# Three passes over 96 MLP units as two full matmuls and one quarter matmul in its own row group, and the last bias added by accumulating transfers

## The chip, the cores and the metric

One core of a Trainium2 chip runs the whole kernel. The metric is the time of one execution on the device in microseconds (us), as the median of several runs. The engines are named as in the profile: PE is the matrix engine (TensorE), PEld its weight loads, DVE the vector engine, ACT the scalar engine, POOL GpSimd, and SP the engine whose queue issues every transfer of the kernel before.

## The reference

`x` is 2048 tokens by 512. The block adds three things: `x`, a linear attention over the normalised `x` with 32 heads, and an MLP over the plain `x` with 1376 hidden units and a squared ReLU.

```
def _A_ref(x, wqkv, wo):
    qkv = ...(x @ wqkv)...
    q, k, v = qkv[0], qkv[1], qkv[2]
    phi = lambda t: jnp.where(t > 0, t + 1, jnp.exp(t)) + 1e-6
    pq, pk = phi(q), phi(k)
    kv = jnp.einsum("bhsd,bhse->bhde", pk, v)
    z = jnp.einsum("bhsd->bhd", pk)
    num = jnp.einsum("bhqd,bhde->bhqe", pq, kv)
    den = jnp.einsum("bhqd,bhd->bhq", pq, z)[..., None] + 1e-6
    o = num / den
    return ... o.reshape(B, S, D) @ wo

def _B_ref(x, w1, b1, w2, b2):
    h = jnp.einsum("bsd,df->bsf", x, w1) + b1
    zero = jnp.zeros_like(h)
    r = jnp.where(h > zero, h, zero)
    h = r * r
    out = jnp.einsum("bsf,fd->bsd", h, w2) + b2
    return out

x = A_x
xn = _layernorm(x, axis=-1)
return x + _A_ref(xn, A_wqkv, A_wo) + _B_ref(xn, B_w1, B_b1, B_w2, B_b2)
```

The last line gives the MLP the normalised `x` as well. The change touches only the second product of the MLP, `h @ w2 + b2`, and there only the last 96 of the 1376 units.

## The kernel before

**Split numbers.** Each 32-bit operand of a large product is held as two fp32r tiles, a high part (the rounded number) and a low part (what rounding left). A product is three matmuls, or passes, into the same PSUM bank: high by high, high by low, low by high (`PASSES`, `three`, lines 122 to 128). The high part is copied by ACT, the low part is a subtraction on DVE (`split`, `rest_of`).

**Tiling.** The 2048 tokens are 16 tiles of 128, in four blocks of four (`TB`). The 1376 units are 11 chunks of 128 (`NF`); chunk 10 has only 96 units (`FL`). In the kernel before, row 96 of chunk 10 carries `b2`: its weight in `w2` is `b2` and its hidden value is 1, because its bias in `b1s` is 1 and its column of `w1` is zero. Rows 97 to 127 are zero. So chunk 10 costs as much as a full chunk.

**Stages.** First the keys and values of all 16 tiles. Then two rounds of a loop over `n`, each for two blocks, `t1` and `t2`. A round computes the hidden units of both blocks at once by a seven-product scheme over pairs of chunks (the loop over `p`, lines 909 to 992). Inside that loop the second MLP product of block `t1` runs too, chunk by chunk, into four PSUM banks `acc`, one for each tile (`mlp_2`): chunk 10 opens the banks at `p == 0`. The hidden units of `t2` wait in `r2`. Then block `t1` gets its attention product (`add_attention`, 12 matmuls a tile), the sum with the residual on DVE (`add`) and its store. After it a loop over `e` (lines 1036 to 1064) takes nine waiting chunks of `t2`, four `add_attention` follow, and the two last chunks, `last_two` (0 and 10), close the banks. In the very last tile of the program the last two chunks go into two separate half banks (`end`, 256 columns each), so that half of the tile can leave while the other half is computed.

**Weights.** `w1` and `w2` are loaded piece by piece into six `raw` buffers. `piece_2` loads 128 rows of `w2`, and returns the two operations that make its high and low part (ACT, then DVE). The list `w2next` holds them, and `next_2`, `high_2` and the loop over `e` run them at fixed places. Chunk 10 of `w2` is loaded and split three times in the program, chunk 10 of `w1` (`raw_1`) twice.

**Order.** The program's text is the order of each engine's queue (`manual_schedule`): an instruction waits in its queue until its inputs are there and its output place is free, and everything behind it on that engine waits too. `hidden_2` squares the hidden units and splits them (ACT, ACT, DVE). `wait_for` does that for a chunk of `r2`. `load_res` loads `x` of a block as the residual, two tiles for each transfer, into `res`.

Of the kernel before, what the change touches and what calls it, by code (L numbers as in the profile page):

```python
# [7 lines left out]
F32 = mybir.dt.float32  # L8
F32R = mybir.dt.float32r
AF = mybir.ActivationFunctionType  # L10
# [8 lines left out]
def kernel(  # L19
# [43 lines left out]
    NP = NF // 2  # L63
    FP = NF * P
    FL = F - (NF - 1) * P
    assert D == 512 and S % BT == 0 and FL % 32 == 0 and FL < P

    nc.scalar.preload_act_table_set("natural_log_exp_and_others")

# [9 lines left out]
    def w512(name, tag, bufs):  # L79
        return work.tile([P, 512], F32, name=name, tag=tag, bufs=bufs)  # L80
# [65 lines left out]
    ident = keep.tile([P, P], F32, name="ident")  # L146
# [23 lines left out]
    def piece_q(j, eh, el):  # L170
        t = raw(f"rq{j}", chunk(wqkv, j, 0, D))
        g4 = lambda ap: ap.rearrange("p (g j c) -> p g j c", g=NJ, j=NJ)
        return lambda: split(g4(wq[0][:, j, :]), g4(wq[1][:, j, :]), gjc(t), eh, el)

    def raw_1(f):
        n = min(P, F - f * P)
        t = w512(f"r1_{f}", "raw", 6)
        tj = t.rearrange("p (j n) -> p j n", j=NJ)
        if n < P:
            nc.gpsimd.memset(tj[:, :, n:], 0.0)  # L180
        nc.sync.dma_start(tj[:, :, :n], w1[:, f * P:f * P + n].rearrange("(j p) n -> p j n", j=NJ))
        return t

    w2r = []
# [7 lines left out]

    def piece_2(f, at):

        if f < NF - 1:
            t = raw(f"r2_{f}", w2[f * P:(f + 1) * P, :])
        else:
            t = w512(f"r2_{f}", "raw", 6)
            nc.gpsimd.memset(t[FL:, :], 0.0)  # L199
            nc.sync.dma_start(t[:FL, :], w2[f * P:, :])  # L200
            nc.sync.dma_start(t[FL:FL + 1, :], b2[None, :])
        w2s[f] = [w2r[at // 2][:, at % 2 * 2 + u] for u in range(2)]
        h, l = w2s[f]
        return [lambda: copy("act", h, t), lambda: rest_of(l, t, h)]


    def group(*tiles):
# [225 lines left out]
    def hidden_2(name, r):  # L433
# [3 lines left out]
        split(s[:, 0], s[:, 1], r, "act", "dve")  # L437
        return s

    def relu(o, i, f):  # L440
        nc.scalar.activation(o, i, AF.Relu, bias=b1s[:, f:f + 1])  # L441

# [14 lines left out]
    def mlp_2(acc, f, s, first=False):  # L457
        for k in range(TB):
            three(acc[k], [s[:, u, k * P:(k + 1) * P] for u in range(2)], w2s[f], first, False)

    def add_attention(acc, i, last=False):
        t = aT.pop(i)
# [29 lines left out]
    nc.gpsimd.memset(b1s[:, NF - 1:], 0.0)  # L492
    nc.gpsimd.memset(b1s[FL:FL + 1, NF - 1:], 1.0)
    groups = {}
    x4, x8 = four("x4", "r1"), four("x8", "r2")
    for i0 in range(0, NT, TB):
# [150 lines left out]
    for i in range(2, NT):  # L647
        if i == NPE:
            wq = both("wq", ("B0", "B1"))
        if i == 3:  # L650
            nc.sync.dma_start(b1s[:, :NF - 1], b1[:(NF - 1) * P].rearrange("(f p) -> p f", p=P))
            nc.sync.dma_start(b1s[:FL, NF - 1:], b1[(NF - 1) * P:, None])
        move()
        fetch()
        ps = pks[i] if i < 3 else bank(f"pk{i}")
        if i > 2:
            project(i, ps, wk, HL)
        high = low = keep_t = lambda: None
        if i + 1 < NDVE:
            high, low, keep_t = transposed(i + 1)  # L660

        soon_turned = transposed(i + 2) if 11 <= i and i + 2 < NT else ()

        def late():
            if soon:
                roots(*soon)
            low()

        phi_k(i, ps, high, late)
        run(*soon_turned)  # L670
        later = normalise(*soon) if soon else []
        parts(i)
        keep_t()
        if i == 2:
            tokens(2)
        if i + 1 < NT:
# [12 lines left out]
        kx(i - 1)  # L689
# [100 lines left out]
    for n in range(2):  # L790
# [100 lines left out]
        t5, res = None, {}  # L891

        def load_res(t):
            for k in range(2):
                r = two(f"res{t}_{k}")
                i = t * TB + 2 * k
                nc.sync.dma_start(r, xf[i * P:(i + 2) * P, :].rearrange("(i p) d -> p i d", i=2))
                for i in range(2):
                    res[t, 2 * k + i] = r[:, i, :]

        def add(ps, t, k, a=0, z=D):
            r = res[t, k]
# [6 lines left out]
        for p in range(NP + 1):  # L909
# [5 lines left out]
                product(A, A11, [x[:, :2] for x in x1], True)  # L915
            if p:
                nc.vector.tensor_tensor(out=t5, in0=before, in1=t5, op=OP.add)
            if 0 < p < NP:
                chunk_split(1, 0, s34)
            if p:  # L920
                relu(r2[fb - 2], t5, fb - 2)
            if p < NP:
                c11 = w512(f"c11_{n}_{p}", "p", 6)
                copy("act", c11, A)
                product(B, A12, [x[:, 2:] for x in x1], True, True)
                high_2()
                nc.vector.tensor_tensor(out=c11, in0=B, in1=c11, op=OP.add)
                relu(c11, c11, fa)
# [15 lines left out]
            t5 = t5_  # L944
            if p == 0:
                T.update({k: tokens_sum(k, f"B{k - 3}") for k in (3, 4)})
                def last_sums(k):
                    for f in (difference_high, difference_low):
                        for j in range(2):
                            f(k, j, o34[k - 3][:, j])  # L950

                last_sums(3)
# [24 lines left out]
            nc.vector.tensor_tensor(out=c12, in0=C, in1=c12, op=OP.add)  # L977
            high_2()
            if p == 0:
                last_sums(4)  # L980
            relu(r2[fa], c12, fa)
            next_2(2 * p + 2)
            if p:
                mlp_2(acc, fb - 2, s.pop(fb - 2))
            else:
                mlp_2(acc, NF - 1, s.pop(NF - 1), True)
            if p == TB - 1:
                do(at1)
                move(16)
            product(A, S3, [T[3][:, u] for u in range(2)])  # L990
            if p == 2:
                load_res(t1)

        def wait_for(f):
            s[f] = hidden_2(f"s{n}_{t2}_{f}", r2[f])

        def sum_2(acc, k, f, first, stop, a=0, z=D):
            three(acc, [s[f][:, u, k * P:(k + 1) * P] for u in range(2)],
                  [w2s[f][u][:, a:z] for u in range(2)], first, stop)

# [35 lines left out]
        for e, f in enumerate(waiting[:-2]):  # L1036
            mlp_2(acc, f, s.pop(f), e == 0)
            if e + 3 < NF - 2:
                wait_for(waiting[e + 3])
            move(4)  # L1040
            if n == 0 and e == 3:
                f2 = xT[t2 - 2] = four(f"xt{t2 - 2}", "r3")
                nc.sync.dma_start(f2, xTd[t2 - 2])
            if e:
                do(w2next, 2)
                if e + 8 < NF:
                    g = waiting[e + 8]
                    w2next.extend(piece_2(g, place(g)))
            if e == 2:
                load_res(t2)  # L1050
            if 0 < e < 5:
                do(columns_todo)
            if e == NF - 6 and n == 0:
                wq = both("wr", ("B0", "B1"))
            if e == NF - 5:
                attention_places("ra", "r1")
                attentions_T(t2 * TB, t2 * TB + 1)
                fetch()
            if e == NF - 4:
                turned = attention_T(t2 * TB + 2)  # L1060
                pieces(1)
            if e == NF - 3:
                run(turned, attention_T(t2 * TB + 3))
                pieces(1)
        for k in range(TB):
            add_attention(acc, t2 * TB + k, n == 1 and k == last)
            if k < 2:
                wait_for(last_two[k])
                pieces(1)
            do(columns_todo)  # L1070
        if n == 1:
            add(acc[last], t2, last)
        for k in range(TB):
            if n == 1 and k == last:
                for a in (0, D // 2):
# [38 lines left out]
```

## Time and profile before

| what | value |
|---|---|
| median of 3 runs | 422.67 us (422.57 to 422.84) |
| the profiled execution, its own time | 422.49 us |
| its span, first to last instruction | 420.8 us |
| granted TensorE clock | 1.000 |
| PE busy | 99% of the span, 1860 matmuls |
| PEld busy | 82% |
| DVE busy | 70% |
| ACT busy | 60% |
| POOL busy | 7% |
| moved by transfers | 46.16 MB, mean 110 GB/s |

How to read it: a busy time of PE overlaps itself, since one matmul begins before the one ahead has drained. The distance from one matmul to the next is therefore read from the chain of waits, where a stretch of matmuls that follow each other is one line: start, length, engine, tile, line and count. Lines of the timeline show start, length, engine, line, operation, output and inputs, count, and in brackets how long the engine was idle before and what ended that. Groups of instructions end with busy us, mean ns of one, and idle time before. An issue of a transfer is shown with its kilobytes and the median time from issue to landing.

### The profile page before, as it was taken

The page shows a single profiled execution, that of the slowest core. Times are in us where ns is not written, and L with a number is a line of the kernel's source. Part 1 is how long each engine was busy: PE and PEld are TensorE (multiplying, and loading weights), DVE is VectorE, ACT ScalarE, POOL GpSimd, SP SyncE. Part 2 cuts the span into 40 slices and gives each one's busy share as a digit, 9 for nine tenths or more (in the row PEclk, how much of TensorE's full clock was granted, in tenths as well). Part 3 has the DMA queues.
Part 4 walks back from the last instruction along what each step waited for, and adds up shares of the span by engine and source line. Part 5 has one row for each costly group of instructions (what it writes and reads, how often), then busy time and mean ns, then how long its engine had stood idle before and what let it go on. Part 6 is the DMA issues. An engine that isn't in the chain of part 4 may idle for free.

```text
span 420.8 us, 5373 instructions
## 1 busy us (share of the span) xinstructions
PE 415.2 (99%) x1860; PEld 343.6 (82%) x1860; DVE 294.2 (70%) x536; ACT 254.0 (60%) x451; POOL 27.6 (7%) x50
## 2 busy tenths in 40 slices
PE   7999999999999999999999999999999999999996
PEld 7788888888887888888888888888888888888885
DVE  6886767777578877677579475586967667577343
ACT  5867777675467767665457362676667665546230
POOL 3242222220000000000000000000000000000000
PEclk9999999999999999999999999999999999999999
DMA  7885422800412231645026652401120654024502
GB/s 240 286 243 157 130 89 92 278 15 3 112 50 77 75 100 26 199 82 169 0 85 191 173 196 97 124 0 50 51 75 25 202 101 149 2 95 97 152 0 100
DMA packets 44818, 46.16 MB, mean 110 GB/s; under 512 B 5716, under 2 KB 31060, under 8 KB 44536
## 3 DMA queue, kind: packets, MB, share of 16 engines
q1 hardware_dynamic: 44792, 45.84, 36.5%
q8 instruction: 14, 0.23, 0.2%
q14 instruction: 12, 0.10, 0.1%
HBM read 32.71 MB, written 8.91 MB: 99 GB/s over the span
## 4 chain that ended last, share of the span: by engine, by line
PE 98%; DVE 1%; DMA 1%; ACT 0%; issue 0%
PE acc L128 39%; PE b L453 23%; PE kx L380 10%; PE pk L361 10%; PE pq L361 10%; PE pz L128 1%; PE b L128 1%; PE pkv L773 1%; PE pm L128 1%; DMA x<-in_A_x_dram 1%; PE pt L300 1%; PE end L128 0%; DVE st L214 0%; DVE xp L253 0%; DVE res L903 0%; ACT xs1h L316 0%
## 5 line engine op out<-in xcount | busy, mean ns | idle before, releaser
L128 PE MATMUL acc<-w2r,s 128*128 128x512 f32 x498 | 116.6, 389 | 0.0
L128 PEld LDWEIGHTS acc<-w2r,s 128*128 128x128 f32 x498 | 93.5, 188 | 19.6
L453 PE MATMUL b<-T,aop 128*128 128x512 f32 x240 | 59.6, 389 | 0.0
L453 PEld LDWEIGHTS b<-T,aop 128*128 128x128 f32 x240 | 45.0, 188 | 9.4
L380 PE MATMUL kx<-pk,tok 128*128 128x512 f32 x192 | 46.8, 392 | 0.0
L380 PEld LDWEIGHTS kx<-pk,tok 128*128 128x128 f32 x192 | 35.6, 188 | 7.9 <-DVE pk L369 0.6
L128 PE MATMUL acc<-mh,aTsr 128*128 128x512 f32 x96 | 30.3, 390 | 0.0
L109 ACT ACTIVATE w2r<-r 128x512 fp32r<-128x512 f32 x32 | 20.0, 625 | 13.8 <-PE acc L128 11.3
L120 DVE TENSOR_TENSOR w2r<-r,w2r 128x512 fp32r<-128x512 f32 x32 | 21.9, 685 | 7.3 <-ACT w2r L109 7.2
L453 PE MATMUL b<-xs0h,aop 128*128 128x512 f32 x80 | 26.4, 391 | 0.0
L117 POOL TENSOR_TENSOR tok<-xp,tok 128x512 fp32r<-128x512 f32 x16 | 21.7, 1362 | 54.9 <-ACT tok L109 54.9
L117 DVE TENSOR_TENSOR s<-c,s 128x512 fp32r<-128x512 f32 x20 | 13.8, 692 | 16.3 <-ACT s L109 16.3
L356 DVE SCALAR_TENSOR_TENSOR q<-pq,q 128x512 f32<-128x512 f32 x16 | 11.0, 689 | 14.9 <-ACT q L354 14.9
L109 ACT ACTIVATE aop<-S 128x512 fp32r<-128x512 f32 x20 | 12.6, 629 | 14.6 <-DVE S L702 9.4
L128 PEld LDWEIGHTS acc<-mh,aTsr 128*128 128x128 f32 x96 | 18.0, 188 | 3.8
L903 DVE TENSOR_TENSOR res<-acc,res 128x512 f32<-128x512 f32 x16 | 11.0, 692 | 14.2 <-PE acc L128 14.2
L352 ACT ACTIVATE q<-pq 128x512 f32<-128x512 f32 x16 | 9.4, 591 | 18.5 <-PE pq L361 18.5
L199 POOL MEMSET r<- 32x512 f32 x3 | 1.6, 522 | 278.2 <-DVE w2r L120 272.3
L128 PE MATMUL acc<-ml,aTsr 128*128 128x512 f32 x48 | 18.7, 390 | 0.0
L453 PEld LDWEIGHTS b<-xs0h,aop 128*128 128x128 f32 x80 | 15.0, 188 | 3.4 <-ACT rz L441 0.3
L453 PE MATMUL b<-xs0l,aop 128*128 128x512 f32 x40 | 15.6, 389 | 0.0
L285 DVE STREAM_TRANSPOSE at<-g 128x512 f32<-128x512 f32 x16 | 10.5, 689 | 6.8 <-DMA g<-q 6.8
(192 smaller groups left out, 826.7 us busy)
## 6 DMA issues: line engine op xcount, KB each, us to landing
r<-in_B_w_dram SPq DMA_DIRECT2D x49, 256.0 KB, 3.2
res<-in_A_x_dram SPq DMA_DIRECT2D x8, 512.0 KB, 5.9
g<-q SPq DMA_DIRECT2D x64, 64.0 KB, 2.1
out_dram<-res SPq DMA_DIRECT2D x15, 256.0 KB, 2.1
x<-in_A_x_dram SPq DMA_DIRECT2D x5, 512.0 KB, 5.6
via<-xp SPq DMA_DIRECT2D x5, 512.0 KB, 2.6
xg<-via SPq DMA_DIRECT2D x20, 128.0 KB, 3.0
xTd<-t SPq DMA_DIRECT2D x8, 256.0 KB, 3.1
```

The costliest lines, as they stand in the source:

```text
L109: nc.scalar.activation(o, i, AF.Copy, bias=bias)
L117: ENG[el].tensor_tensor(out=l, in0=src, in1=f32(h), op=OP.subtract)
L120: nc.vector.tensor_tensor(out=l, in0=src, in1=f32(h), op=OP.subtract)
L128: nc.tensor.matmul(ps, lhsT=a[u], rhs=b[v], start=first and n == 0, stop=last and n == 2)
L285: nc.vector.transpose(o.rearrange("p j (r t) -> p r j t", r=NJ), G.rearrange("p r (j c) -> p r j c", j=NJ))
L300: nc.tensor.transpose(t[k][:, at:at + P], xp[i][:, j * P:(j + 1) * P], ident)
L352: nc.scalar.activation(p, ps, AF.Relu, scale=-1.0)
L356: nc.vector.scalar_tensor_tensor(p, ps, 0.0, p, op0=OP.max, op1=OP.add)
L361: nc.tensor.matmul(ps, lhsT=cols(i)[u][:, j, slot(i)], rhs=w[v][:, j, :], start=first and n == 0, stop=last and n == len(steps) - 1)
L380: nc.tensor.matmul(kxp[c], lhsT=tok[i][:, u, c * P:(c + 1) * P], rhs=pk[i][:, v], start=i == 0 and (u, v) == first, stop=i == NT - 1 and ( ...
L453: nc.tensor.matmul(ps, lhsT=a[u][:, j * P:(j + 1) * P], rhs=b[v][:, j, :], start=first and j == 0 and n == 0, stop=last and j == 1 and n == 2,
L903: nc.vector.tensor_tensor(out=r[:, a:z], in0=ps, in1=r[:, a:z], op=OP.add)
```

## The change

The 96 units are three groups of 32: A (units 0 to 31 of the chunk), B and C. Three passes over 96 rows are 288 rows; the change lays them out as two full matmuls of 128 rows and one of 32.

- Chunk 10 is loaded in another order (`units`): B and C on partitions 0 to 63, A on 64 to 95, and A once more on 96 to 127. This holds for `w1`, `w2` and `b1`, each in three transfers.
- `w2`: the tile `h` holds the high part of B, C and A, and on 96 to 127 the low part of A. The tile `l` holds the low part of B and C, and on 64 to 127 their high part, copied by POOL. A new tile `w2q` holds the high part of A four times, once in each group of 32 partitions, by four POOL copies.
- hidden units (`hidden_last`): `h` is the high part of all 128 rows; `hl` has the high part of B and C on 0 to 63 (a POOL copy) and their low part on 64 to 127 (DVE); `lq` has the low part of A, tile `k` of the block on partitions 32k to 32k+31 (four DVE subtractions of 32 by 128).
- `last_2` does the two full matmuls for a tile. `quarters_2` does the third part for the four tiles of a block: four matmuls of 32 rows, each in its own group of 32 rows of the array, into the four different banks.
- `b2` is no longer a row of chunk 10. After a block's residual is loaded, POOL issues four accumulating transfers (`add_bias`), each adding `b2` to one tile of it.
- In the closing part chunk 10 is prepared before chunk 0, the four pieces of `wq` come one with each `add_attention`, and at the start of the loop over `p` the parts of `T[4]` and one `next_2` are moved from `p == 0` to `p == 1`.

```diff
     def raw_1(f):
-        n = min(P, F - f * P)
         t = w512(f"r1_{f}", "raw", 6)
         tj = t.rearrange("p (j n) -> p j n", j=NJ)
-        if n < P:
-            nc.gpsimd.memset(tj[:, :, n:], 0.0)
-        nc.sync.dma_start(tj[:, :, :n], w1[:, f * P:f * P + n].rearrange(...))
+        for a, o, n in units(f):
+            nc.sync.dma_start(tj[:, :, a:a + n], w1[:, o:o + n].rearrange("(j p) n -> p j n", j=NJ))
         return t
+    def units(f):
+        if f < NF - 1:
+            return [(0, f * P, P)]
+        return [(0, f * P + Q, 2 * Q), (2 * Q, f * P, Q), (3 * Q, f * P, Q)]
     def piece_2(f, at):
+        h, l = w2s[f] = [w2r[at // 2][:, at % 2 * 2 + u] for u in range(2)]
...
-            nc.gpsimd.memset(t[FL:, :], 0.0)
-            nc.sync.dma_start(t[:FL, :], w2[f * P:, :])
-            nc.sync.dma_start(t[FL:FL + 1, :], b2[None, :])
...
+        for a, o, n in units(f):
+            nc.sync.dma_start(t[a:a + n], w2[o:o + n, :])
+        def high():
+            w2s["q"] = w2q = work.tile([P, D], F32R, name="w2q", tag="rb")
+            copy("act", h, t)
+            copy("pool", l[2 * Q:], h[:2 * Q])
+            for k in range(TB):
+                copy("pool", w2q[k * Q:(k + 1) * Q], h[2 * Q:3 * Q])
+        def low():
+            rest_of(l[:2 * Q], t[:2 * Q], h[:2 * Q])
+            rest_of(h[3 * Q:], t[3 * Q:], h[3 * Q:])
+        return [high, low]
+    def hidden_last(name, r):
+        nc.scalar.activation(r, r, AF.Square)
+        s = pair(name)
+        h, hl = s[:, 0], s[:, 1]
+        lq = keep.tile([P, P], F32R, name=f"{name}q", tag="ident")
+        copy("act", h, r)
+        copy("pool", hl[:2 * Q], h[:2 * Q])
+        def rests():
+            rest_of(hl[2 * Q:], r[:2 * Q], h[:2 * Q])
+            for k in range(TB):
+                at, to = slice(2 * Q, 3 * Q), slice(k * P, (k + 1) * P)
+                rest_of(lq[k * Q:(k + 1) * Q], r[at, to], h[at, to])
+        return (h, hl, lq), rests
+    def last_2(ps, k, s, first, stop, a=0, z=D):
+        for u in range(2):
+            nc.tensor.matmul(ps, lhsT=s[u][:, k * P:(k + 1) * P], rhs=w2s[NF - 1][u][:, a:z],
+                             start=first and u == 0, stop=stop and u == 1)
+    def quarters_2(acc, s):
+        for k in range(TB):
+            at = slice(k * Q, (k + 1) * Q)
+            nc.tensor.matmul(acc[k], lhsT=s[2][at], rhs=w2s["q"][at], start=False, stop=False)
...
-            nc.sync.dma_start(b1s[:FL, NF - 1:], b1[(NF - 1) * P:, None])
+            for a, o, n in units(NF - 1):
+                nc.sync.dma_start(b1s[a:a + n, NF - 1:], b1[o:o + n, None])
...
-        s = {NF - 1: hidden_2(f"sz{n}", rz)}
+        sz, sz_rests = hidden_last(f"sz{n}", rz)
+        s = {}
+        if n:
+            sz_rests()
...
+        def add_bias():
+            def to(r):
+                for i in range(2):
+                    nc.gpsimd.dma_start(r[:, i], b2[None, :].partition_broadcast(P), accum_op=OP.add)
+            todo = [lambda r=r: to(r) for r in biased]
+            biased.clear()
+            return todo
...
+            if p == 1:
+                last_sums(4, difference_low)
...
+            if p == 1:
+                next_2(2)
...
+                if n == 0:
+                    sz_rests()
...
+            if p == NP - 1:
+                do(bias, 2)
...
             if p == 0:
-                last_sums(4)
+                last_sums(4, difference_high)
             relu(r2[fa], c12, fa)
-            next_2(2 * p + 2)
             if p:
+                next_2(2 * p + 2)
                 mlp_2(acc, fb - 2, s.pop(fb - 2))
             else:
-                mlp_2(acc, NF - 1, s.pop(NF - 1), True)
+                for k in range(TB):
+                    last_2(acc[k], k, sz, True, False)
+                quarters_2(acc, sz)
...
+            if p == 3:
+                bias = add_bias()
...
+            if e == 4:
+                bias = add_bias()
+            if e in ((5, 6) if n else (7, 8)):
+                do(bias)
...
         for k in range(TB):
+            if n == 1 and k == last:
+                quarters_2(acc, s[NF - 1])
             add_attention(acc, t2 * TB + k, n == 1 and k == last)
             if k < 2:
-                wait_for(last_two[k])
-                pieces(1)
+                wait_for(last_two[1 - k])
+            pieces(1)
             do(columns_todo)
         if n == 1:
             add(acc[last], t2, last)
+        else:
+            quarters_2(acc, s[NF - 1])
```

More of the change, by code (lines that the diff above doesn't have):

```diff
@@ L65 @@
     FL = F - (NF - 1) * P
-    assert D == 512 and S % BT == 0 and FL % 32 == 0 and FL < P
+    Q = P // TB
+    assert D == 512 and S % BT == 0 and FL == 3 * Q
     nc.scalar.preload_act_table_set("natural_log_exp_and_others")
@@ L145 @@
     w2s, wos = {}, {}
-    ident = keep.tile([P, P], F32, name="ident")
+    ident = keep.tile([P, P], F32, name="ident", tag="ident")
     heads = work.tile([P, P], F32, name="heads", tag="heads")
@@ L173, in piece_q @@
         return lambda: split(g4(wq[0][:, j, :]), g4(wq[1][:, j, :]), gjc(t), eh, el)
+    def units(f):
+        if f < NF - 1:
+            return [(0, f * P, P)]
+        return [(0, f * P + Q, 2 * Q), (2 * Q, f * P, Q), (3 * Q, f * P, Q)]
     def raw_1(f):
-        n = min(P, F - f * P)
         t = w512(f"r1_{f}", "raw", 6)
         tj = t.rearrange("p (j n) -> p j n", j=NJ)
-        if n < P:
-            nc.gpsimd.memset(tj[:, :, n:], 0.0)
-        nc.sync.dma_start(tj[:, :, :n], w1[:, f * P:f * P + n].rearrange("(j p) n -> p j n", j=NJ))
+        for a, o, n in units(f):
+            nc.sync.dma_start(tj[:, :, a:a + n], w1[:, o:o + n].rearrange("(j p) n -> p j n", j=NJ))
         return t
@@ L193, in piece_2 @@
     def piece_2(f, at):
+        h, l = w2s[f] = [w2r[at // 2][:, at % 2 * 2 + u] for u in range(2)]
         if f < NF - 1:
             t = raw(f"r2_{f}", w2[f * P:(f + 1) * P, :])
[L197 to L200, printed above, removed]
-            nc.sync.dma_start(t[FL:FL + 1, :], b2[None, :])
-        w2s[f] = [w2r[at // 2][:, at % 2 * 2 + u] for u in range(2)]
-        h, l = w2s[f]
-        return [lambda: copy("act", h, t), lambda: rest_of(l, t, h)]
+            return [lambda: copy("act", h, t), lambda: rest_of(l, t, h)]
+        t = w512(f"r2_{f}", "raw", 6)
+        for a, o, n in units(f):
[10 more added lines that the diff above has]
+        return [high, low]
     def group(*tiles):
@@ L491 @@
                                 channel_multiplier=sign)
-    nc.gpsimd.memset(b1s[:, NF - 1:], 0.0)
-    nc.gpsimd.memset(b1s[FL:FL + 1, NF - 1:], 1.0)
     groups = {}
@@ L890 @@
         r2 = {f: r2[k // 4][:, k % 4] for k, f in enumerate(waiting)}
-        t5, res = None, {}
+        t5, res, biased = None, {}, []
         def load_res(t):
@@ L899, in load_res @@
                     res[t, 2 * k + i] = r[:, i, :]
+                biased.append(r)
+        def add_bias():
[5 more added lines that the diff above has]
+            return todo
         def add(ps, t, k, a=0, z=D):
@@ L946, with last_sums @@
                 T.update({k: tokens_sum(k, f"B{k - 3}") for k in (3, 4)})
-                def last_sums(k):
-                    for f in (difference_high, difference_low):
+                def last_sums(k, *what):
+                    for f in what:
                         for j in range(2):
                             f(k, j, o34[k - 3][:, j])
-                last_sums(3)
+                last_sums(3, difference_high, difference_low)
             if p or n:
@@ L992 @@
                 load_res(t1)
+            if p == 3:
+                bias = add_bias()
         def wait_for(f):
-            s[f] = hidden_2(f"s{n}_{t2}_{f}", r2[f])
+            name = f"s{n}_{t2}_{f}"
+            if f < NF - 1:
+                s[f] = hidden_2(name, r2[f])
+            else:
+                s[f], rests = hidden_last(name, r2[f])
+                rests()
         def sum_2(acc, k, f, first, stop, a=0, z=D):
+            if f == NF - 1:
+                last_2(acc, k, s[f], first, stop, a, z)
+                return
             three(acc, [s[f][:, u, k * P:(k + 1) * P] for u in range(2)],
@@ L1060 @@
                 turned = attention_T(t2 * TB + 2)
-                pieces(1)
             if e == NF - 3:
                 run(turned, attention_T(t2 * TB + 3))
-                pieces(1)
         for k in range(TB):
+            if n == 1 and k == last:
+                quarters_2(acc, s[NF - 1])
             add_attention(acc, t2 * TB + k, n == 1 and k == last)
             if k < 2:
-                wait_for(last_two[k])
-                pieces(1)
+                wait_for(last_two[1 - k])
+            pieces(1)
             do(columns_todo)
@@ L1072 @@
             add(acc[last], t2, last)
+        else:
+            quarters_2(acc, s[NF - 1])
         for k in range(TB):
```

## Prediction

> **What bounds the kernel now.** I read the page's totals and its chain of waits first.
>
> ```profile
> span 420.8 us, 5373 instructions
> PE 415.2 (99%) x1860; PEld 343.6 (82%) x1860; DVE 294.2 (70%) x536; ACT 254.0 (60%) x451; POOL 27.6 (7%) x50
> PE 98%; DVE 1%; DMA 1%; ACT 0%; issue 0%
> ```
>
> PE holds 98% of the chain that ended last, and waits for nothing that matters. A change pays here only if it takes work off PE, and costs only if it adds work there or makes PE wait. Next the chain of waits in order of time (start, length, engine, tile, line, count), for PE's price of one matmul and for the places of chunk 10.
>
> ```profile
> 108.36 3.57 PE pkv L773 x32
> 138.19 2.72 PE acc L128 x12
> 206.19 54.60 PE acc L128 x240
> 294.79 2.72 PE acc L128 x12
> 362.79 53.24 PE acc L128 x234
> 416.03 1.44 PE end L128 x12
> 417.50 0.42 DVE res L903
> ```
>
> A matmul over 512 columns takes 2.72 / 12 = 0.227 us of PE, one over 256 columns in the last tile 1.44 / 12 = 0.120. Chunk 10 opens block `t1`'s banks at 138.19 and 294.79. For `t2` it stands at the end of the two long stretches. Of the 240 matmuls from 206.19 the last 24 (chunks 0 and 10) begin at 206.19 + 216 x 0.2275 = 255.3 and the 48 of the attention at 244.4. Of the 234 from 362.79 the last 18 begin at 411.9 and the attention at 401.0.
>
> How long a single matmul and a single weight load last is in the groups by form (last two numbers of the first field: busy us, mean ns).
>
> ```profile
> L128 PE MATMUL acc<-w2r,s 128*128 128x512 f32 x498 | 116.6, 389 | 0.0
> L128 PEld LDWEIGHTS acc<-w2r,s 128*128 128x128 f32 x498 | 93.5, 188 | 19.6
> ```
>
> A matmul lasts 389 ns but the next begins after 227, so 389 - 227 = 162 ns of each lies under the next one. No matmul of 32 rows stands anywhere in this trace.
>
> **What is removed from PE.** Each of the four blocks loses the third pass of chunk 10, four matmuls. Fifteen of the sixteen are full: 15 x 0.227 = 3.40 us. The last tile's is two half ones: 2 x 0.120 = 0.24. Together -3.64 us, all on the path.
>
> **What is added to PE.** Four quarters of 32 rows in each block, 16 in all, each still over 512 columns. Call the time of one set of four q.
> - If all four run side by side, q is one matmul and three issue gaps. The gap is what a matmul costs beyond its columns: 0.227 for 512 and 0.120 for 256 leave 2 x 0.120 - 0.227 = 0.013. So q = 0.227 + 3 x 0.013 = 0.27.
> - If they follow each other, q = 4 x 0.227 = 0.91, and nothing is gained.
> - In between the weight loads set the pace. The product for `pkv` has moving sides of only 128 columns and comes at 3.57 / 32 = 0.112 us each, so a load takes no more than that. Four loads at that distance with the matmuls side by side give q = 3 x 0.112 + 0.227 = 0.56.
> - Below 0.27 nothing can go; above 0.91 there is a drain of PE on the way into the quarters and out, 0.162 each by the rows above, so 1.23 at most.
>
> I take 0.56: the loads are separate instructions, and the matmul ahead leaves room for about one of them. The same value comes out when the quarters run side by side and PE drains on both sides, 0.27 + 2 x 0.162 = 0.59. The sum is -3.64 + 4 x 0.56 = -1.40 us.
>
> The Trainium skill, "TensorE: Matmul & The Clock Gate", section "Measured speedup vs the span model", has four row tiles at 512 columns at 3.07 times; an estimate from that page is q = 0.91 / 3.07 = 0.30 and a sum of -2.46. No run here shows it yet.
>
> **DVE, ACT and POOL beside it.** Chunk 10's low parts cost DVE one subtraction more for each `w2` load, and four small ones for each block. ACT's count stays.
>
> ```profile
> L117 DVE TENSOR_TENSOR sz<-rz,sz 128x512 fp32r<-128x512 f32 x2 | 1.4, 686 | 1.8 <-ACT sz L109 1.8
> L401 DVE TENSOR_SCALAR den<-den 128x32 f32<-128x32 f32 x16 | 2.9, 182 | 0.6
> L702 DVE TENSOR_TENSOR S<-r 128x256 f32<-128x256 f32 x10 | 4.2, 418 | 0.0
> ```
>
> A subtraction of 32 by 128 lies between 0.18 and 0.42, by width nearer to 0.25; four are about 1.0 us. With 0.69 for the `w2` one it is 3 x 0.69 + 4 x 1.0 = 6 us of DVE in all. Is it hidden? The tight place is `p == 0` of the first round, in the timeline of ACT and DVE:
>
> ```profile
> 130.36 0.63 ACT L109 ACTIVATE sz<-rz 128x512 fp32r<-128x512 f32 x1
> 130.90 0.61 ACT L109 ACTIVATE w2r<-r 128x512 fp32r<-128x512 f32 x1
> 135.20 1.30 DVE L120 TENSOR_TENSOR T<-Tf,T 128x512 fp32r<-128x512 f32 x2 [1.20 <-ACT T L109]
> 137.48 0.69 DVE L117 TENSOR_TENSOR s<-c,s 128x512 fp32r<-128x512 f32 x1 [0.98 <-ACT s L109]
> 144.22 0.68 DVE L117 TENSOR_TENSOR aop<-S,aop 128x512 fp32r<-128x512 f32 x1
> ```
>
> The new subtractions come behind the one that ends at 136.5: the large one ends near 137.1 and the small ones near 138.1, while PE opens the banks at 138.2, wants `hl` one pass later and `lq` after eight, near 140. They fill the idle 0.98 and push DVE back by some 0.6; in exchange the two subtractions of `T[4]` and one of `w2` go behind the start of `p == 1`. There `T[4]`'s low part is due at the fourth product of `p == 1`, (138.2 + 18 x 0.227) + 18 x 0.227 - 0.35 = 146.0; the `aop` of 144.22 had these two and the `w2` one ahead of it, now it and the `w2` one follow them, so DVE is done with them near 144.2. So nothing is late; without that cover each late microsecond would cost one. In the second round chunk 10 has 9 us from its PSUM result to 294.8. I cost it at nothing.
>
> POOL's copies are of a kind that the trace lacks; the nearest rows:
>
> ```profile
> L117 POOL TENSOR_TENSOR tok<-xp,tok 128x512 fp32r<-128x512 f32 x16 | 21.7, 1362 | 54.9 <-ACT tok L109 54.9
> L199 POOL MEMSET r<- 32x512 f32 x3 | 1.6, 522 | 278.2 <-DVE w2r L120 272.3
> ```
>
> One copy c lies between 0.52 (nothing read) and 1.36 (two operands read), say 0.9. In the first round six of them follow the ACT copies of 130.4 and 130.9: they end between 134.5 and 139.4, and the quarters need the last at 140. They fit even at the upper end.
>
> **Transfers.** SP issues two more for `b1s`, two more for each `w1` chunk 10, and three for each `w2` chunk 10 where there were two.
>
> ```profile
> 26.85 1.20 SPq L652 DMA_DIRECT2D b1s<-in_B_b_dram  x1
> 28.67 1.75 SPq L281 DMA_DIRECT2D xg<-via  x4
> 35.47 0.70 DVE L285 STREAM_TRANSPOSE t<-xg 128x512 f32<-128x512 f32 x1
> xg<-via SPq DMA_DIRECT2D x20, 128.0 KB, 3.0
> 40.36 2.72 PE pk L361 x12
> 262.31 23.08 SPq L181 DMA_DIRECT2D r<-in_B_w_dram  x7
> 389.03 1.20 SPq L200 DMA_DIRECT2D r<-in_B_w_dram  x1
> 391.56 2.54 SPq L281 DMA_DIRECT2D g<-q  x4
> 397.65 1.30 DVE L285 STREAM_TRANSPOSE at<-g 128x512 f32<-128x512 f32 x2 [3.45 <-DMA g<-q]
> 399.06 1.29 DVE L120 TENSOR_TENSOR aTsra<-at,aTsra 128x512 fp32r<-128x512 f32 x2
> ```
>
> For `b1s`, `xg` goes out up to 2 x 1.2 = 2.4 us later; of 35.47 - 30.4 = 5.0 us to its reader its landing takes 3.0, so DVE may get it 0.4 late, and PE, which multiplies that tile at 40.36, 4.2 after the transpose, does not. For `w2`, the queue is held up by between nothing and 1.2 us ahead of the last four `g<-q`, for which DVE waits 3.45 us; the first low part is then ready by 399.7 + 1.2 = 400.9, and PE reads it in its third pass at 401.0 + 0.45. Covered, with about half a microsecond left at the worst. `w1` is wanted 17 us after its issue. These are nothing.
>
> `b2` itself goes by POOL's queue, and no such transfer stands in the trace. One issue d is bounded below by an SP issue, 0.45 (0.90 for two), and above by the landing of a residual load, 5.9.
>
> ```profile
> res<-in_A_x_dram SPq DMA_DIRECT2D x8, 512.0 KB, 5.9
> 390.62 0.90 SPq L897 DMA_DIRECT2D res<-in_A_x_dram  x2
> 399.53 0.61 ACT L109 ACTIVATE w2r<-r 128x512 fp32r<-128x512 f32 x1
> 411.94 0.69 DVE L903 TENSOR_TENSOR res<-acc,res 128x512 f32<-128x512 f32 x1 [6.01 <-PE acc L128]
> ```
>
> In the last block POOL waits for the residual (landing by 391.5 + 5.9 = 397.4), issues four, and only then makes the five copies for chunk 10 of `w2`, which themselves wait for ACT at 400.1. The quarters come ahead of the fourth attention, at 401.0 + 36 x 0.2275 = 409.2. With d = 1.0 POOL is through at 401.4 + 5 x 0.9 = 405.9, and the sums that need `b2` come at 411.9. I cost it at nothing; the cover is 3.3 us, and beyond it PE waits one for one. In the first round's `t2` the copies go first (ACT at 242.8 to 243.4), then four issues, then the copy into `hl`: 243.4 + 4.5 + 4.0 + 0.9 = 252.8 against PE's need near 256.8. For the `t1` blocks the issues go out at `p == 4`, ten and more microseconds ahead of their sums.
>
> The closing part has its pieces in another order on ACT and DVE. Behind them ACT waits long:
>
> ```profile
> 263.55 0.60 ACT L352 ACTIVATE q<-pq 128x512 f32<-128x512 f32 x1 [8.46 <-PE pq L361]
> ```
>
> Its list is done near 255.1 and `wq` is wanted at 260.8; the new subtractions add 1.0 us on DVE. Nothing again.
>
> **Sum.** On the profiled execution, 422.49 us (its span 420.8 and 1.7 around it): 422.49 - 1.40 = 421.09. That execution lies 0.18 under the median of the runs, so the forecast is 421.3.
>
> **The rivals.**
> - *Full overlap.* q = 0.27, sum -3.64 + 1.08 = -2.56, time 420.1. For it: weight loads run ahead of matmuls all through the trace. Against: one load of 188 ns for each matmul of 227 leaves little room for three more.
> - *Drains on top.* The quarters paced by their loads and PE emptied on both sides: q = 0.56 + 2 x 0.162 = 0.89, sum -3.64 + 3.55 = -0.09, time 422.6: no change. For it speaks that the array must change from one tile of 128 rows to four of 32, and back; the trace has no such change. The Trainium skill, "TensorEngine Tiling (Array Packing)", "Key Properties", says that changing the tiling mode drains TensorE; whether that holds here no row shows.
> - *The row groups do not overlap.* The change does not do what it says: q = 0.91 + 0.32 = 1.23, sum -3.64 + 4.92 = +1.28, time 423.9, slower. It decides from q above 1.1.
> - *POOL becomes the wait.* PE stands at the quarters of the last block until `w2q` is copied behind four slow issues. It decides from 397.4 + 4d + 5c = 409.2, so from d = 1.8 at c = 0.9 and 1.2 at c = 1.36. At d = 2.5 and c = 1.36 POOL ends at 414.2: a wait of 5.0, less 1.4 from the rest, time 426.3. It outweighs the gain from a wait of 1.4. For it: nothing bounds d closely. Against: POOL is busy 7% of the span, so only this work itself can queue there.
>
> **How the numbers follow.** Chances: the forecast 0.37, full overlap 0.15, drains 0.18, no overlap 0.13, POOL 0.17. The likeliest one's own range runs from q = 0.45 to 0.70: 420.8 to 421.8. What a measurement can tell is 0.2%, 0.85 us, so faster means under 421.8. Faster: 0.37 + 0.15 = 0.52; same: 0.18; slower: 0.13 + 0.17 = 0.30. The range goes from full overlap, 419.9, to no overlap, 424.1; it leaves out most of the POOL case and little else.
>
> **What will show it.** In the chain, 138.19's twelve become eight and four quarters, and the start of what follows gives q directly: 8 x 0.227 + q after the opening. Starts of the quarters 0.11 apart confirm the loads' pace; 0.01, the overlap; 0.23, none. A gap on either side is a drain. Idle time of PE ahead of a quarter released by POOL shows the last rival, and by DVE that the small subtractions are not covered. An idle DVE at L903 ending with a transfer into `res` shows `b2` late. The prediction is wrong if q is above 0.70 or below 0.45, or if PE gets idle time at any of these places.

## The result and the profile after

| | median | executions | ratio to before, 95% interval |
|---|---|---|---|
| before | 422.62 us | 16 | |
| changed | 421.76 us | 16 | 0.9982 (0.9974 to 0.9991) |

The kernel is 0.86 us faster; by the interval between 0.4 and 1.1. The forecast was 421.3, 1.40 faster.

The totals of the page and the chain of waits of the changed kernel, at the places that the prediction read before:

```profile
span 420.7 us, 5470 instructions
PE 414.1 (98%) x1859; PEld 340.6 (81%) x1859; DVE 304.9 (72%) x555; ACT 253.0 (60%) x451; POOL 55.2 (13%) x78
3.62 6.65 DMA x<-in_A_x_dram
109.07 3.57 PE pkv L820 x32
138.90 1.84 PE acc L500 x8
140.73 0.43 PE acc L507 x3
141.16 7.04 PE b L489 x30
148.21 2.72 PE acc L129 x12
206.69 49.11 PE acc L129 x216
255.80 0.44 PE acc L507 x3
261.00 21.76 PE pq L379 x96
295.00 1.81 PE acc L500 x8
304.29 2.72 PE acc L129 x12
362.77 46.39 PE acc L129 x204
416.95 0.25 PE end L500 x2
417.22 0.42 DVE res L964
```

The span of this one execution is only 0.1 us shorter. That is its start: a transfer of `x` lands at 3.62 + 6.65 = 10.3, and `pkv` begins at 109.07, where it began at 108.36 before. From there to the last sum it is 417.22 - 109.07 = 308.15, against 417.50 - 108.36 = 309.14: 0.99 less. The start scatters by such amounts from run to run (`pkv` begins at 108.40 in e6 below, which has the same program up to there), so below the stretches behind it are compared.

From the opening of the banks to the next chunk the kernel before has 12 + 30 matmuls, which take 9.52 us at 0.2267 each. Now it is 148.21 - 138.90 = 9.31 and 304.29 - 295.00 = 9.29, for 8 + 30 full matmuls (8.62) and one set. So a set costs q = 0.69 and 0.67, and the block gains 0.21 and 0.23. The two `t2` blocks show it in their whole stretch. The first took 54.60 and takes 261.00 - 206.69 = 54.31. The last took 417.47 - 362.79 = 54.68, up to the end of its last matmul, and takes 417.20 - 362.77 = 54.43. That is 0.29 and 0.25 gained, q = 0.62 and 0.67. The four gains add up to 0.98, so the sets explain the 0.99.

PEld's timeline shows what a set is (start, length, operation, count, idle before), then the tile `w2q`'s instructions with the length of one in ns (least, median, most):

```profile
138.51 1.80 PEld L500 LDWEIGHTS acc<-w2r,sz 128*128 128x128 f32 x8
140.66 0.19 PEld L507 LDWEIGHTS acc<-w2q,sz0q 32*128 32x128 f32 x4 [0.35 <-issue]
141.10 1.22 PEld L489 LDWEIGHTS b<-T,aop 128*128 128x128 f32 x6 [0.24 <-issue]
```

```profile
L507 PE MATMUL acc<-w2q,sz0q x4: 490/496/498, 140.7 to 140.7; 32*128 32x512 f32 x4
L507 PEld LDWEIGHTS acc<-w2q,sz0q x4: 181/181/181, 140.7 to 140.7; 32*128 32x128 f32 x4
```

All four loads lie within 0.19 us, where one takes 0.181: they run side by side, as do the four matmuls (all begin at 140.7). But PEld stands idle 0.35 ahead of them and 0.24 behind them, waiting for nothing that the profile shows. The matmuls' starts show where the time goes: the last full one starts at 140.34, the quarters at 140.66, the next two full ones at 141.10 and 141.43. These distances of 0.32, 0.44 and 0.33 are 0.09, 0.21 and 0.11 more than the usual 0.227, 0.41 in all.

### The profile page after: what moved, and what is told of

Read it like the earlier page. It is cut to its first block, busy times and chain, and to the rows that moved or that the text cites. A ratio compares the mean times of both kernels' runs of the same rounds, so it can differ in the third digit from the quotient of the medians.

```text
span 420.7 us, 5470 instructions
## 1 busy us (share of the span) xinstructions
PE 414.1 (98%) x1859; PEld 340.6 (81%) x1859; DVE 304.9 (72%) x555; ACT 253.0 (60%) x451; POOL 55.2 (13%) x78
## 4 chain that ended last, share of the span: by engine, by line
PE 96%; DMA 2%; DVE 1%; SPq 1%; issue 0%
PE acc L129 36%; PE b L489 23%; PE kx L398 10%; PE pq L379 10%; PE pk L379 9%; PE acc L500 2%; DMA x<-in_A_x_dram 2%; PE pz L129 1%; PE b L129 1%; PE pkv L820 1%; PE pm L129 1%; PE pt L318 0%; PE acc L507 0%; SPq L527 0%; SPq L157 0%; PE end L129 0%
## 5 line engine op out<-in xcount | busy, mean ns | idle before, releaser
L129 PE MATMUL acc<-w2r,s 128*128 128x512 f32 x477 | 112.8, 389 | 0.0
L129 PEld LDWEIGHTS acc<-w2r,s 128*128 128x128 f32 x477 | 89.5, 188 | 18.9 <-issue 0.2
L956 POOL DMA_DIRECT2D res<-in_B_b_dram x16 | 14.1, 1067 | 150.5 <-DMA res<-in_A_x_dram 57.5
L121 DVE TENSOR_TENSOR w2r<-r,w2r 128x512 fp32r<-128x512 f32 (+2 forms) x35 | 25.4, 725 | 7.3 <-ACT w2r L110 7.2
```

Source lines behind the costliest of these rows:

```text
L121: nc.vector.tensor_tensor(out=l, in0=src, in1=f32(h), op=OP.subtract)
L129: nc.tensor.matmul(ps, lhsT=a[u], rhs=b[v], start=first and n == 0, stop=last and n == 2)
L956: nc.gpsimd.dma_start(r[:, i], b2[None, :].partition_broadcast(P), accum_op=OP.add)
```

## The experiments

All ratios are to the kernel before, run on the same chip. e1 to e4 shared one set of its runs (median 422.50), e5 to m1 a second (422.52), f1 to m2 a third (422.54). The last column is the stretch of the profiled execution from the start of `pkv` to the start of the last sum; the kernel before has 309.14 there and the changed one 308.15.

| run | median us | ratio (95%) | `pkv` to last sum |
|---|---|---|---|
| e1_full_third | 422.92 | 1.0007 (0.9998 to 1.0016) | 309.36 |
| e2_no_third | 419.02 | 0.9921 (0.9901 to 0.9941) | 305.65 |
| e3_double | 422.70 | 1.0009 (0.9996 to 1.0021) | 308.97 |
| e4_one_quarter | 421.69 | 0.9985 (0.9972 to 0.9999) | 308.09 |
| e5_bias_late | 422.48 | 0.9996 (0.9987 to 1.0004) | 309.06 |
| e6_no_bias | 422.13 | 0.9989 (0.9981 to 0.9998) | 308.41 |
| e7_bias_alone | 427.95 | 1.0125 (1.0102 to 1.0147) | 315.63 |
| f1_pieces_early | 421.73 | 0.9979 (0.9967 to 0.9990) | 308.14 |
| f2_bias_alone_pieces_late | 422.49 | 0.9999 (0.9990 to 1.0008) | 309.13 |
| f3_bias_early | 421.71 | 0.9978 (0.9965 to 0.9992) | 308.13 |
| m1_merged | 420.97 | 0.9963 (0.9951 to 0.9975) | 307.98 |
| m2_merged | 420.93 | 0.9966 (0.9951 to 0.9981) | 307.39 |

**What a set costs.** The theory by then was "side by side with a change of shape"; its main rival the forecast's, "loads set the pace". Four kernels change only `quarters_2`.

> The four quarter matmuls of a set become four matmuls of 128 rows (all four groups at once), so PE never changes its tile shape; each of a block's four tiles gets the sum of the four tiles' corrections. Theory 'side by side': in the changed kernel a set costs 0.67 us, of which 0.23 is one matmul and 0.44 the change of shape and back; here a set costs 4 x 0.227 = 0.91 with no gap around it, so +0.24 a set, +0.96 in all: 422.7, level with the kernel before. Rival 'loads set the pace' (the forecast's): also 0.91, 422.7, but then the weight loads of the changed kernel's quarters must stand 0.11 apart. Rival 'the gain comes from the other edits' (b2 by transfers, the new order): it stays at 421.8.

```diff
-            at = slice(k * Q, (k + 1) * Q)
-            nc.tensor.matmul(acc[k], lhsT=s[2][at], rhs=w2s["q"][at], start=False, stop=False)
+            nc.tensor.matmul(acc[k], lhsT=s[2], rhs=w2s["q"], start=False, stop=False)
```

> The quarter matmuls are left out (the low part of the hidden units of group A times the high part of w2 is missing); their inputs are still prepared. It measures q. 'Side by side with a change of shape', q = 0.67: 421.76 - 4 x 0.67 = 419.1. The forecast's q = 0.56: 419.5. Full overlap without a change of shape, q = 0.27: 420.7.

```diff
     def quarters_2(acc, s):
-        for k in range(TB):
...
+        return
```

> Each set runs its four quarters twice (eight matmuls of 32 rows; the correction is added twice). 'Side by side': the second four run in the same shape and cost one matmul more, 0.23 to 0.27 a set: +0.9 to +1.1, 422.8. 'Loads set the pace': four more loads at 0.112, +0.45 a set: +1.8, 423.6. If a row group cannot load while its own matmul runs, the second four start only when the first have drained, +0.40 to 0.66 a set: 423.4 to 424.4.

```diff
-        for k in range(TB):
+        for k in [*range(TB)] * 2:
```

> Only the first of the four quarters of each set is kept (three of four tiles lack the correction of group A). 'Side by side': the set still costs a change of shape and one matmul, so only some 0.02 a set is saved: 421.7. 'Loads set the pace': 3 x 0.112 a set is saved, 1.3 in all: 420.4.

```diff
-        for k in range(TB):
+        for k in range(1):
```

The same stretch of the chain, from the opening of the second round's banks to the next chunk, of e2, e4, e3 and e1 in this order:

```profile
292.74 1.81 PE acc L500 x8
294.55 6.85 PE b L489 x30
301.40 2.72 PE acc L129 x12
```

```profile
294.22 1.81 PE acc L500 x8
296.03 0.43 PE acc L507
303.50 2.72 PE acc L129 x12
```

```profile
294.85 1.81 PE acc L500 x8
296.66 0.66 PE acc L507 x5
304.33 2.72 PE acc L129 x12
```

```profile
294.99 1.81 PE acc L500 x8
296.80 0.94 PE acc L506 x4
304.58 2.72 PE acc L129 x12
```

| in the set | stretch | over e2 |
|---|---|---|
| nothing (e2) | 8.66 | 0 |
| one quarter (e4) | 9.28 | 0.62 |
| four quarters (the change) | 9.29 | 0.63 |
| eight quarters (e3) | 9.48 | 0.82 |
| four full matmuls (e1) | 9.59 | 0.93 |

One quarter costs what four cost, so the loads set no pace: that theory wanted a third of a microsecond less for each set in e4, 1.3 in all, and e4 stayed at 421.69. Four more quarters cost 0.19, about one matmul. Leaving the sets out takes 421.76 - 419.02 = 2.74 off, 0.69 a set; the two stretches from `pkv` on differ by 2.50, 0.62 a set. A set is thus one matmul's time, 0.23, and some 0.40 to 0.46 that does not depend on how many quarters there are. e1 shows that the packing makes the gain: with the same kernel otherwise, but four full matmuls, the time is back at the kernel before (1.0007); it lies 0.2 above the 422.7 expected, within its interval.

**The way of b2.** Here "covered" stood against POOL or the transfers being a limit.

> The last block's b2 transfers are issued at e = 7 and 8, behind POOL's copies for chunk 10 of w2, instead of 5 and 6: the second part of the change undone. 'Covered': POOL makes its five copies from 400.8 to 404.7, then the four issues (0.88 us each, one pause of 2.0) to about 410, landing some 5 us later, near 414 for the last. DVE's first sum of the last block (at 412.6, which needs that tile) then waits 1 to 2 us, and the end comes 0.3 to 0.6 later: 422.1 to 422.4. PE does not wait. Rival 'POOL is no limit either way': 421.8.

```diff
-            if e in ((5, 6) if n else (7, 8)):
+            if e in (7, 8):
```

POOL and DVE of e5 in the timeline, at the end of the last block:

```profile
401.73 3.32 POOL L114 CAST w2q<-w2r 32x512 fp32r<-32x512 f32 x4
405.00 2.61 POOL L956 DMA_DIRECT2D res<-in_B_b_dram  x3
409.24 0.87 POOL L956 DMA_DIRECT2D res<-in_B_b_dram  x1 [1.62 <-issue]
```

```profile
414.55 2.48 DVE L964 TENSOR_TENSOR res<-acc,res 128x512 f32<-128x512 f32 x4 [6.30 <-PE acc L500]
416.95 0.75 DVE L964 TENSOR_TENSOR res<-end,res 128x256 f32<-128x256 f32 x2
```

The first sum comes at 414.55. Its bank closed with the fourth attention, and the changed kernel sums it at 412.6, in an execution whose `pkv` began 0.76 later; so the sum is some 2.7 late, where 1 to 2 were expected. The profile puts the wait down to PE, but the sum also needs the transfer issued at 409.24, which landed 5.2 later, at 414.4. All four sums and the two halves then follow without a gap, the last from 417.3 on. 422.48 is just above the expected 422.1 to 422.4 and not distinguishable from the kernel before; from `pkv` to the last sum 0.91 of the 0.99 is lost. With the transfers behind the copies in the last block the change would lose most of its gain.

> The accumulating transfers are left out, so b2 is missing from the output. 'Covered': they cost nothing, 421.8. If POOL's queue or the 4.2 MB of transfers delay anything on PE's path: lower, by up to the idle time of PE that the profile would show.

```diff
             def to(r):
-                for i in range(2):
-                    nc.gpsimd.dma_start(r[:, i], b2[None, :].partition_broadcast(P), accum_op=OP.add)
+                pass
```

It takes 422.13, no lower than the changed kernel; its profile has one wait of 0.4 us of PEld for an attention part (`aTsra`) that the changed kernel lacks. The transfers, as placed, cost nothing that these runs can tell.

> The kernel before with only the b2 part: b2 leaves chunk 10's spare row and goes to the residuals by the same POOL transfers; three passes as before. 'Packing alone makes the gain': level with the kernel before, 422.6. Rival 'the b2 part gives some of it': lower than 422.4. If the transfers cost something that the packing hides: above 422.8.

```diff
-    nc.gpsimd.memset(b1s[FL:FL + 1, NF - 1:], 1.0)
...
-            nc.sync.dma_start(t[FL:FL + 1, :], b2[None, :])
...
+            if e == 4:
+                bias = add_bias()
+            if e in ((5, 6) if n else (7, 8)):
+                do(bias)
```

(with `biased`, `add_bias` and the calls in the loop over `p` as in the change.) By the medians it is 5.4 us slower (its six executions lie between 425.40 and 429.32): the third case of the expectation, with a size that nobody had forecast. First the timelines of POOL, SP and ACT near the end of the first round, then the chain of waits there. PE's longest wait follows (total, times, longest), and last three stretches: start and end, length, busy us of PE, PEld, DVE, ACT, POOL with counts, then granted clock, transfer share, GB/s.

```profile
237.10 1.75 POOL L904 DMA_DIRECT2D res<-in_B_b_dram  x2 [10.81 <-DMA res<-in_A_x_dram]
239.87 0.85 POOL L904 DMA_DIRECT2D res<-in_B_b_dram  x1 [1.03 <-DMA res<-in_A_x_dram]
241.77 0.88 POOL L904 DMA_DIRECT2D res<-in_B_b_dram  x1 [1.05 <-DMA g<-q]
241.31 2.42 SPq L162 DMA_DIRECT2D rq<-in_A_wqkv_dram  x4
251.11 0.63 ACT L109 ACTIVATE wrh<-rq 128x512 fp32r<-128x512 f32 x1 [5.64 <-DMA rq<-in_A_wqkv_dram]
253.12 0.63 ACT L109 ACTIVATE aTsr<-at 128x512 fp32r<-128x512 f32 x1 [1.38 <-DVE at L284]
```

```profile
241.31 9.78 DMA rq<-in_A_wqkv_dram
251.11 0.64 ACT wrh L109
251.77 0.69 DVE wrl L117
252.46 0.62 DVE at L284
253.08 0.58 DVE aTsr L120
253.71 8.34 PE acc L128 x23
```

```profile
PE acc L128 <- DVE aTsr L120: 3.4, 1, 3.4
```

```profile
250.50:252.50 2.00, 0.00 (x0) 0.00 (x0) 0.73 (x2) 0.63 (x1) 0.00 (x0) 1.00 0.44 170
253.50:259.50 6.00, 5.79 (x14) 4.55 (x15) 5.14 (x9) 5.94 (x12) 0.00 (x0) 0.50 0.00 1
260.00:266.00 6.00, 6.00 (x27) 4.88 (x26) 2.22 (x5) 0.00 (x0) 0.00 (x0) 1.00 0.12 44
```

The four accumulating transfers go out just ahead of `wq`'s pieces. Those land 9.8 us after their issue (ACT had the first 5.1 us after issue in the kernel before; the 4.2 in the next expectation is too low). ACT waits for the first of them, DVE waits for ACT with that piece's low part, and behind the low part in DVE's queue stands the transposition `at` of an attention part; ACT's copy of that part, at 253.12, waits for `at` too. PE waits 3.4 us for it, and then works for some 6 us at a granted clock of 0.50, which costs it another 3. Together that is about the 6.4 us by which this execution, at 428.97, is longer than the median before. In the changed kernel two things differ: POOL's copies for chunk 10 stand ahead of the transfers, so they go out from 248.6, and `wq`'s pieces come behind the attention copies. Three more kernels tell these apart.

> The changed kernel with the four pieces of wq at their old places: two ahead of the last attention copies (e = 7 and 8), two with the first two add_attention. Found in e7: b2's transfers, issued at 237 to 242.6, hold wq's up until 251.1 (4.2 us from issue before, 9.8 there), ACT waits for wq in its queue ahead of an attention copy, and PE waits for that. Theory 'POOL's copies keep the transfers apart': here b2 goes out only from 248.6, wq lands near 246, so nothing waits: 421.8. Rival 'the moved pieces are what saves the changed kernel': a wait of PE near 250 and 425 or more.

```diff
             if e == NF - 4:
                 turned = attention_T(t2 * TB + 2)
+                pieces(1)
             if e == NF - 3:
                 run(turned, attention_T(t2 * TB + 3))
+                pieces(1)
...
                 wait_for(last_two[1 - k])
-            pieces(1)
+                pieces(1)
```

> e7_bias_alone with the four pieces of wq moved to the four add_attention, as in the change. wq still lands near 251, but no attention copy stands behind it on ACT. If that queue is the cause of e7's 428: no wait of PE for aTsr, level with the kernel before, 422.6. If the transfers themselves are the cost: above 424.

The opposite edit, in e7_bias_alone.

> The changed kernel with b2's transfers at e = 5 and 6 in the first round too. They go out at some 238 to 243 and wq lands near 251 as in e7; the pieces stand late on ACT, so only the last chunk's hidden units and wq are held up, which PE needs at 256 and 260: 421.8 to 422.3, PE waiting at most some tenths. If it goes to 424 or more, the place of the transfers matters by itself.

```diff
-            if e in ((5, 6) if n else (7, 8)):
+            if e in (5, 6):
```

In f2 `wq` is as late as in e7. These are ACT's attention copies in f2 and its first copy of `wq` in f2, f3 and f1:

```profile
243.98 1.23 ACT L109 ACTIVATE aTsr<-at 128x512 fp32r<-128x512 f32 x2 [1.47 <-DVE at L284]
250.63 0.63 ACT L109 ACTIVATE wrh<-rq 128x512 fp32r<-128x512 f32 x1 [4.24 <-DMA rq<-in_A_wqkv_dram]
251.17 0.63 ACT L110 ACTIVATE wrh<-rq 128x512 fp32r<-128x512 f32 x1 [3.54 <-DMA rq<-in_A_wqkv_dram]
246.42 0.61 ACT L110 ACTIVATE wrh<-rq 128x512 fp32r<-128x512 f32 x1
```

The attention copies are done before ACT waits, and the time is the kernel before's, 0.9999. f1 and f3 are level with the change (421.73, 421.71): in f3 the transfers go out early and `wq` is late, in f1 they go out from 247.5 and ACT waits for no piece. So either cover is enough here: the wait came only with early transfers and the pieces ahead of the copies together. Whether ordinary transfers of the same size would delay `wq` as much, no run tells.

**Two sets next to each other.** If the change of shape is the cost, two sets side by side save one of it.

> The two sets of a round run next to each other, ahead of the last chunk of block t1: the quarters of t1, then those of t2, which open t2's banks; w2q is made once and kept, and for its room the p buffers are five instead of six. Two changes of shape are saved. 'Side by side with a change of shape': 0.44 saved for each, 0.88 in all: 420.9. 'Loads set the pace': nothing saved, 421.8. If five p buffers or the early subtractions make PE wait, it shows as idle time of PE in the loop over p, and the time is higher by that.

```diff
             if p == 2:
                 load_res(t1)
+                lq2 = early_q(f"sq{n}", r2[NF - 1])
...
+        acc2 = [bank(f"acc{t2}_{k}") for k in range(TB)]
+        quarters_2(acc, sz[2])
+        quarters_2(acc2, lq2, True)
         for k in range(TB):
             three(acc[k], [s1[:, u, k * P:(k + 1) * P] for u in range(2)], w2s[f], False, True)
```

(`early_q` squares chunk 10 of `t2` there and makes its four small low parts; the calls of `quarters_2` at the old places go; `w2q` is a tile of its own, and the `p` buffers are five.) It takes 420.97, as expected: faster than the kernel before, and by the medians 0.79 faster than the changed one, though the two intervals just touch.

> m1_merged with the low part of the first round's chunk 10 made 1.3 us sooner on DVE (ahead of the parts of T[3]) and the four small subtractions after the next hidden chunk. m1's profile lost 0.4 us where PE waited for that low part at 138.7. If it is regained: 420.5; if something else on DVE then comes late: 420.9 as m1 or more.

```diff
             if p == 0:
                 T.update({k: tokens_sum(k, f"B{k - 3}") for k in (3, 4)})
...
+                if n == 0:
+                    sz_rests[0]()
                 last_sums(3, difference_high, difference_low)
...
+            if p == 0 and n == 0:
+                sz_rests[1]()
```

(against m1; the old calls go.) m1's profile had PE waiting once for `sz`, 0.4 us; m2's has no such wait, but the median is the same, 420.93. Between the two profiled executions the gain is there: 307.39 from `pkv` to the last sum, against 307.98. But m1's profiled execution is the slowest of its five, 421.39, 0.42 above their median, and m2's began `pkv` 0.49 later than m1's. So the wait may have stood in that one execution alone; without traces of the others this stays open.

## Why the prediction was right, and where not

- **What bounds it, and what is removed.** Right: PE alone decides, a matmul is worth 0.227, and e1 gives the removed ones back.
- **The price of a set.** This step was off: q was put at 0.56 because "the loads are separate instructions, and the matmul ahead leaves room for about one of them". The loads run side by side and set no pace (0.112 was the distance from one `pkv` matmul to the next; a single load lasts 0.181), and the four sets cost 0.62 to 0.69, 0.66 on average. Of the 0.54 by which the forecast missed, 4 x (0.66 - 0.56) = 0.40 is this; the rest lies within the interval. The mechanism that the prediction named second, side by side with PE drained on both sides, 0.59, fits the runs, 0.07 too small: it reckoned 2 x 0.162 = 0.32 for the two sides, and the starts in the timeline give 0.41. That the two reasons gave nearly the same number was luck. The forecast came close with the wrong one in front, and it took e4 to tell them apart. The ends of the range, 419.9 and 424.1, lie 0.2 outside the times of the two rivals that they are named after, 420.1 and 423.9, and the prediction gives no reason for it.
- **The rival "drains on top"** had the drain right, and lost its case through the loads that it kept. The Trainium skill, "TensorEngine Tiling (Array Packing)", "Key Properties", has the rule that changing the tiling mode drains TensorE; the idle 0.35 and 0.24 of PEld agree with it, and m1, which saves two changes, gains 0.79 of the 0.88 so reckoned. What the runs show by themselves is that a price of some 0.40 is paid once for each set of 32-row matmuls, and next to none in e1, where the matmuls keep 128 rows (0.93 for four, where four times 0.227 is 0.91).
- **The rival "row groups do not overlap"** fell with e4.
- **The rival "POOL becomes the wait".** Not as placed. In the last block three errors cancel: the issues begin at 396.4 and not 397.4, four of them take 5.5 and not 4.0 (one takes 0.88, and ahead of the fourth there is a pause of 2.0), and the five copies take 4.0 and not 4.5. So POOL is through with the copies at 405.9, as forecast, and PE needs them at 409.2. In the first round they do not cancel: POOL's last copy ends at 255.3 and not 252.8, 1.9 ahead of the matmul that reads it, where the prediction had 4.0. With the transfers behind the copies (e5) the cover is gone, and DVE's sums are late, not PE.
- **DVE.** A small subtraction takes 0.28 to 0.36, inside 0.18 to 0.42. Each `w2` load has two subtractions, 0.68 and 1.03, so it costs 1.0 more than before and not 0.69; PE waits for none of them.
- **The closing part's order** was costed at nothing. f1, with `wq`'s pieces at their old places, is level with the change; the rest of the new order had no run of its own, but PE has no wait there. What the prediction missed is the place where the new transfers meet `wq`: it priced POOL's queue, but not what 256 KB accumulating transfers do to loads in flight. e7 puts that at 5.4 us where neither cover stands.

## What to carry to other kernels

Here row groups pay by the set: the change of shape costs about two matmuls of 512 columns (0.40 to 0.46 against 0.227), whether one quarter or four follow, so as many small matmuls as possible belong next to each other. Where a new transfer is added, look for the loads that are in flight at that time, and for what stands behind their reader on its engine. Compare stretches between the same two events rather than spans when the start of the kernel scatters by as much as the change is worth.

## What the runs showed of the hardware

- Four loads of 32 rows in different row groups take 0.19 us together, eight of them 0.30 (e3); the matmuls of one set all begin at the same tenth.
- In e7 PE waited 3.4 us, and from 253.5 to 259.5, the 6 us from about its restart on, the granted clock was 0.50; from 260 it was 1.00 again. The Trainium skill, "TensorE: Matmul & The Clock Gate", "What's actually happening", has the clock fall to half after about 3.4 us of idleness. The half agrees. The time is shorter here: the wait began near 250.3, and from 253.0 to 253.5, before it ended, the clock was already 0.50.
- POOL pauses about 2 us between the third and the fourth accumulating transfer in the changed kernel's last block (1.6 in e5), released by nothing that the profile shows to be needed. Why is open.
